# Holding a DMA queue for four loads, and moving two small loads behind the matmuls, in a long-convolution and MLP kernel

## The chip, the cores and the metric

The program runs on one core of one Trainium2 chip. A core has a matrix engine (TensorE, PE in the profile, with its weight loads as PEld), three engines for elementwise work (VectorE or DVE, ScalarE or ACT, GpSimd or POOL) and a queue engine (SyncE or SP). All of them run their own list of instructions in order and wait for each other through semaphores. SP, ACT and POOL can start DMAs; a DMA is issued by an instruction in the engine's own list, and whatever stands behind that instruction waits until it has been accepted. The metric is the time of one execution on the device in microseconds (us), lower is better.

## The reference

The inputs are a sequence of 2048 positions with 640 channels, all in float32. What is computed:

```python
mod = (silu(c) @ w_mod).reshape(1, 6, 1, 640)
sa, ca, ga, sb, cb, gb = (mod[:, i] for i in range(6))
h = layernorm(x) * (1 + ca) + sa                 # x is A_q
# A: short causal convolution of k (4 taps), times v, then a causal
#    convolution over all 2048 positions with ssm_k (by FFT of length 4096)
kv = shift_conv(k, shift_k) * v
y  = irfft(rfft(kv, 4096) * rfft(ssm_k, 4096))[:2048] + kv * ssm_D
x  = x + ga * (h * y)
h  = layernorm(x) * (1 + cb) + sb
# B: dense layer, squared relu, dense layer (640 -> 1728 -> 640)
x  = x + gb * (relu(h @ w1 + b1) ** 2 @ w2 + b2)
```

## The kernel before, in words

The 640 channels are worked on in five blocks of 128 (the loop `for b in range(NB)`). In each block the long convolution is done as a transform in two steps on TensorE. `unit_a(b, i, g)` (matmuls at L354) is the first step, on a quarter g of the block, for the filter (i = 1, tile half `pt[b][:, 1]`) or for the product kv (i = 0, `pt[b][:, 0]`). `early_h` and `front` (matmuls at L369) are the second step; `front` also multiplies the two spectra (DVE L140, POOL L143 and L146). `back` (L435), `unit_t` (L499) and `unit_y` (L510) go back to positions. While one block goes through the second step and back, the first step of the next block, the short convolution of the block after it (`kv_k`, `kv_s`, `kv_v`, `kv_m`) and the layernorm statistics (`stats1`) are placed between its matmuls. After the five blocks comes the MLP, with PE nearly filled.

The kv of a block is computed with channels on partitions and written to a DRAM tile `kv_d` (L257), and read back by `load_x(b, n)` (L204) in another layout, in n pieces; one piece has as many rows as one call of `unit_a(b, 0, g)` needs. So in block 0, with four pieces, the four calls `unit_a(0, 0, g)` can begin one after the other as the pieces land. The same holds for block 1; blocks 2 to 4 load theirs in one piece. `load_h` (L196) brings the filter, `load_gb` and `load_gi` (L798, L330) the tables of the two steps, `kv_load` (L216) the rows of k and v, `part_load` (L308) rows of `w_mod` and `q_load` (L915) rows of q.

Nearly all DMAs are issued by SP, in the order of the program text; this order, like that of every engine, is fixed by `keep_order` at the end. An entry of a table (`at(FS(b, j), ...)`, `at(GS(b, s), ...)`) says at which of the 28 places of a block a piece of work is put; equal places keep the order in which they were entered. ACT issues a few small ones itself: taps, one table and parts of `ssm_D` at the start, then `c` (tile `ct`, L849) and the table `ca` of the last step (`ca_d`, L850). In the program text these two stand between the last `early_h` of the prologue and the four calls `unit_a(0, 0, g)`, whose results ACT copies out of PSUM (L135). `c` is first read by `mod_start` at place GS(0, 0), the table by `unit_y` at GS(0, 3).

The text of the prologue around the change, in order: `load_x(0, 4)`, `unit_a(0, 1, 3)`, `load_gb(3)`, two pairs of `kv_load` with `load_gi`, `load_h(1)`, two more `load_gi`, six `early_h`, the two DMAs on ACT, four `unit_a(0, 0, g)`. In block 1 `load_x(1, 4)` stands at GS(0, 6), and the next DMA of SP behind it is `part_load(2, 1)` at the same place.

## Time and profile before

| | us |
|---|---|
| median of three runs | 711.5 |
| lowest and highest of them | 709.77, 716.64 |
| the profiled execution | 714.4 |
| its span, first to last instruction | 712.6 |
| PE busy in the span | 669.5 (94%) |
| PE weight loads busy | 639.2 (90%) |
| DVE, ACT, POOL busy | 335.7, 330.7, 295.5 |

The mean clock granted to TensorE in that execution is 0.983 of full speed. In the profile's second part the span is cut into 40 slices of some 17.8 us; a digit is a busy share in tenths. PE stands at 9 in nearly all slices from the sixth on, and is lower in the first five (6, 5, 9, 8, 9); the DMA engines stand at 9, 8, 7, 7, 7 there, and are nearly idle in the last third. The three runs lie 1% apart. The first 100 us are the part in which the change lies; all times of events below are counted from the start of the span.

### The profile page before, as it was taken

To read this page: it belongs to the slowest core of one execution; us is meant where nothing else is said; L and a number is where in the kernel's file an instruction comes from. 1 tells how busy PE (TensorE), PEld (TensorE's weight loads), DVE (VectorE), ACT (ScalarE), POOL (GpSimd) and SP (SyncE) were. 2 spreads that over 40 slices of the span, in tenths; PEclk is the share of its full clock that TensorE was granted. 3 is DMA by queue.
4 is the path that set the end of the run, shared out by engine and by line. 5 is a ranking of instruction groups with operands and counts; after the bars stand their busy time and mean duration, and the time that the engine had idled before them with its cause. 6 is when DMAs were issued, how large, how long until landed. Compare 5 with 4: busy or idle time off the path is not lost.

```text
span 712.6 us, 21026 instructions
## 1 busy us (share of the span) xinstructions
PE 669.5 (94%) x9164; PEld 639.2 (90%) x9164; DVE 335.7 (47%) x661; ACT 330.7 (46%) x685; POOL 295.5 (41%) x338
## 2 busy tenths in 40 slices
PE   6598989979899989999999999999999999999997
PEld 5587878769789879789999999999999999999996
DVE  5255755746887588769831232222312313312313
ACT  4426545766883896557533323323333333233221
POOL 1042026147944977933542522422514415325213
PEclk9989989999999999999999999999999999999999
DMA  9877795969475275238320020020020110200101
GB/s 250 239 209 236 210 271 165 257 184 247 101 194 150 69 207 153 78 89 243 106 73 3 1 75 1 1 75 1 3 75 1 38 38 1 75 1 1 39 1 38
DMA packets 88721, 74.76 MB, mean 105 GB/s; under 512 B 19250, under 2 KB 73906, under 8 KB 88628
## 3 DMA queue, kind: packets, MB, share of 16 engines
q1 hardware_dynamic: 86672, 72.86, 36.1%
q8 instruction: 72, 1.18, 0.7%
q10 hardware_dynamic: 1892, 0.54, 0.3%
q14 instruction: 21, 0.17, 0.1%
q0 software_dynamic: 64, 0.01, 0.0%
HBM read 58.98 MB, written 14.42 MB: 103 GB/s over the span
## 4 chain that ended last, share of the span: by engine, by line
PE 79%; DVE 9%; ACT 4%; DMA 3%; issue 2%; POOL 2%; SPq 0%; DVEq 0%; POOLq 0%; ACTq 0%
PE acc L763 26%; PE h L693 25%; PE x L369 5%; PE qp L435 4%; PE h L369 4%; DVE KV L239 3%; PE y L510 3%; PE pa L354 3%; PE t L499 1%; PE h L684 1%; PE xtp L658 1%; PE kt L227 1%; ACT KV L468 1%; ACT q L135 1%; DVE s L270 1%
## 5 line engine op out<-in xcount | busy, mean ns | idle before, releaser
L140 POOL TENSOR_TENSOR mtmp<-mtmp 128x256 f32<-128x256 f32 x112 | 72.1, 643 | 242.3 <-ACT mtmp L725 234.5
L693 PE MATMUL h<-xt,w_S 128*128 128x256 f32 x1290 | 166.9, 281 | 0.2 <-DVE w_S L146 0.2
L693 PEld LDWEIGHTS h<-xt,w_S 128*128 128x128 f32 x1290 | 161.2, 190 | 0.4 <-DVE w_S L146 0.4
L763 PE MATMUL acc<-w_S,hring 128*128 128x320 f32 x960 | 156.8, 311 | 0.2 <-DVE hring L146 0.2
L146 DVE TENSOR_TENSOR hring<-mtmp,hring 128x256 fp32r<-128x256 f32 x112 | 64.9, 579 | 189.9 <-ACT hring L135 189.8
L763 PEld LDWEIGHTS acc<-w_S,hring 128*128 128x128 f32 x960 | 141.8, 188 | 0.7 <-DVE hring L146 0.7
L725 ACT ACTIVATE mtmp<-h,b1t 128x256 f32<-128x256 f32 x104 | 49.4, 475 | 177.8 <-PE h L693 172.3
L135 ACT ACTIVATE hring<-mtmp 128x256 fp32r<-128x256 f32 x112 | 46.7, 417 | 46.1 <-POOL mtmp L140 44.6
L354 PE MATMUL pa<-wx,p 64*64 64x64 f32 x2560 | 52.3, 232 | 13.9 <-DMA p<-kv_d 3.8
L354 PEld LDWEIGHTS pa<-wx,p 64*64 64x64 f32 x2560 | 45.9, 145 | 21.6 <-issue 11.6
L135 ACT ACTIVATE a<-pa 128x512 f32<-128x512 f32 x80 | 43.7, 604 | 28.9 <-PE pa L354 28.9
L510 PE MATMUL y<-wx,wx 128*64 128x64 f32 x1280 | 47.1, 227 | 6.5 <-ACT wx L135 4.9
L140 DVE TENSOR_TENSOR wx<-x,wx 128x512 f32<-128x512 f32 x64 | 40.8, 681 | 25.3 <-PE x L369 14.6
L510 PEld LDWEIGHTS y<-wx,wx 128*64 128x64 f32 x1280 | 41.7, 140 | 11.4 <-ACT wx L135 5.7
L146 POOL TENSOR_TENSOR we<-wx 128x256 f32<-128x256 f32 x20 | 15.9, 793 | 79.9 <-DVE wx L140 77.9
L369 PE MATMUL x<-a,gb 128*64 128x128 f32 x640 | 44.1, 283 | 1.2 <-ACT a L135 1.1
L143 POOL TENSOR_TENSOR wm<-wm,wm 128x640 f32<-128x640 f32 x20 | 31.8, 1590 | 28.5 <-ACT wm L312 28.3
L660 DVE TENSOR_SCALAR we<-xtp,cbs 128x256 f32<-128x256 f32 x35 | 19.0, 543 | 51.8 <-PE xtp L658 51.8
L239 DVE SCALAR_TENSOR_TENSOR KV<-kt,tap,KV 128x511 f32<-128x511 f32 (+2 forms) x48 | 35.4, 738 | 15.1 <-ACT ktail L135 13.1
L369 PEld LDWEIGHTS x<-a,gb 128*64 128x64 f32 x640 | 38.5, 143 | 2.1 <-ACT a L135 1.3
L135 ACT ACTIVATE q<-qp 128x512 f32<-128x512 f32 (+1 forms) x40 | 21.3, 584 | 35.2 <-PE qp L435 35.2
L369 PE MATMUL h<-a,gb 128*64 128x128 f32 x512 | 36.2, 285 | 0.0
(140 smaller groups left out, 1029.6 us busy)
## 6 DMA issues: line engine op xcount, KB each, us to landing
wm<-in_w_mod_dram SPq DMA_DIRECT2D x25, 320.0 KB, 5.1
KV<-in_A_k_dram SPq DMA_DIRECT2D x20, 256.0 KB, 5.3
KV<-in_A_v_dram SPq DMA_DIRECT2D x20, 256.0 KB, 4.2
xp<-in_A_q_dram SPq DMA_DIRECT2D x5, 1024.0 KB, 9.5
out_dram<-x SPq DMA_DIRECT2D x14, 320.0 KB, 2.9
w1s<-in_B_w_dram SPq DMA_DIRECT2D x13, 320.0 KB, 3.7
w2s<-in_B_w_dram SPq DMA_DIRECT2D x13, 320.0 KB, 3.6
kv_d<-KV SPq DMA_DIRECT2D x16, 256.0 KB, 4.0
```

The source lines that it names most:

```text
L135: act.activation(o, i, AF.Copy)
L140: eng.tensor_mul(o, a, b)
L143: eng.tensor_add(o, a, b)
L146: eng.tensor_sub(o, a, b)
L239: dve.scalar_tensor_tensor(o, x, tap[:, b, t : t + 1], o, op0=ALU.mult, op1=ALU.add)
L354: pe.matmul(t[e][64 * r : 64 * r + 64, g].rearrange("p m d -> p (m d)"), pt[b][l, i, 8 * q + g, :], cw[l, r], start=True, stop=True,)
L369: pe.matmul(t[64 * a : 64 * a + 64, s + r], gb[:, g, r, a], AX[b][i][:, 2 * g + a], start=True, stop=True,)
L435: pe.matmul(t[a][:, u], gi[l, 4 * j + u, r], w[r][l, u % 2], start=(r == 0), stop=(r == 1),)
L510: pe.matmul(y[64 * h : 64 * h + 64, 4 * (g % 2) + i].rearrange("p c l d -> p (c l d)"), tss[g][:, i, 64 * r : 64 * r + 64], ca[:, r, h], s ...
L693: pe.matmul(hps[n, f][:m], WI[1, f][:, a, b], XT[n][:, x, b], start=(b == 0 and i == 0), stop=(b == NB - 1 and i == 2),)
L725: act.activation(r[:m], h[:m], AF.Relu, bias=b1t[:m, f : f + 1])
L763: pe.matmul(acc[2 * s + i], h[:, a, s * P : (s + 1) * P], w[:, y, i * 320 : (i + 1) * 320], start=(f == 0 and ti == 0), stop=(f == NF - 1 ...
```

## The change

Three things change.

1. All DMAs of SP go through a new function `sp_dma`. It issues the DMA, and when the list `behind` holds a name, the DMA just issued gets a dependence on that earlier instruction, with a semaphore: it is not issued before the named DMA has landed.
2. `load_x` puts the name of its third piece (index 2 of four) in that list for blocks 0 and 1. So the next DMA of SP after each of these two loads waits until three quarters of x have landed, and everything behind it in SP's order waits too. In block 0 that DMA is `load_gb(3)`, in block 1 it is `part_load(2, 1)`. The fourth piece is issued ahead of the wait.
3. The DMAs of `c` and of the last table stand behind the four `unit_a(0, 0, g)` in ACT's order, not ahead of them.

```diff
+HOLD = {0: 2, 1: 2}
...
+    behind = []
+
+    def sp_dma(o, i):
+        sp.dma_start(o, i)
+        if behind:
+            info = mybir.DependencyInfo(mybir.DependencyClass.Sync, mybir.DependencyReason.DATA)
+            tc.add_manual_dep(nc.cur_bb.bb.instructions[-1], behind.pop(), info, reason="place in time")
...
     def load_x(b, n=1):
         w = DG // n
         for i in range(n):
-            sp.dma_start(
+            sp_dma(
                 pt[b][:, 0, i * w : (i + 1) * w],
                 xsrc[:, b * DG + i * w : b * DG + (i + 1) * w, :],
             )
+            if i == HOLD.get(b):
+                held = nc.cur_bb.bb.instructions[-1].name
+        if b in HOLD:
+            behind.append(held)
...
     for j in range(6):
         early_h(0, j)
+    for g in range(4):
+        unit_a(0, 0, g)
     act.dma_start(ct, c.rearrange("o (b p) -> p (o b)", p=P))
     act.dma_start(ca, ca_d.rearrange("p (r h n) -> p r h n", r=2, h=2))
-    for g in range(4):
-        unit_a(0, 0, g)
```

All other `sp.dma_start` of the kernel become `sp_dma` with the same arguments.

More of the change, by code (lines that the diff above doesn't have):

```diff
@@ L203, in load_x @@
         for i in range(n):
-            sp.dma_start(
+            sp_dma(
                 pt[b][:, 0, i * w : (i + 1) * w],
@@ L215, in kv_load @@
         for w, src in ((0, k), (1, v)):
-            sp.dma_start(t[:, w], src[rows, cols].rearrange("(t p) d -> p t d", p=P))
+            sp_dma(t[:, w], src[rows, cols].rearrange("(t p) d -> p t d", p=P))
     kt = {}
@@ L256, in kv_m @@
         dve.tensor_mul(acc, kt[1], acc)
-        sp.dma_start(kv_d[b * P : (b + 1) * P, h * 512 : (h + 1) * 512], acc)
+        sp_dma(kv_d[b * P : (b + 1) * P, h * 512 : (h + 1) * 512], acc)
     st1 = sb.tile([P, NL, 2], F32, tag="st1", name="st1")
@@ L307, in part_load @@
         t = parts[j, b] = sb.tile([P, D], F32, tag="STG", name=f"wm_{j}_{b}", bufs=4)
-        sp.dma_start(t, w_mod[b * P : (b + 1) * P, j * D : (j + 1) * D])
+        sp_dma(t, w_mod[b * P : (b + 1) * P, j * D : (j + 1) * D])
     def part_scale(j, b):
@@ L329, in load_gi @@
         src = gi_d.rearrange("p (g r n) -> p g r n", g=16, r=2)
-        sp.dma_start(gi[:, 4 * i : 4 * i + 4], src[:, 4 * i : 4 * i + 4])
+        sp_dma(gi[:, 4 * i : 4 * i + 4], src[:, 4 * i : 4 * i + 4])
     AX, QT = {}, {}
@@ L457, in load_xp @@
         t = sb.tile([P, NL, P], F32, tag=f"XP{b % 2}", name=f"xp_{b}")
-        sp.dma_start(t, q[:, b * P : (b + 1) * P].rearrange("(l p) d -> p l d", p=P))
+        sp_dma(t, q[:, b * P : (b + 1) * P].rearrange("(l p) d -> p l d", p=P))
         XPt[b] = t
@@ L546, in finish_add @@
         add(pool, x[:, js], x[:, js], u[:, js])
-        sp.dma_start(
+        sp_dma(
             x1_d[4 * j * P : (4 * j + 4) * P, b * P : (b + 1) * P].rearrange("(l p) d -> p l d", p=P),
@@ L572, in w_load @@
         if kind == 1:
-            sp.dma_start(
+            sp_dma(
                 s[:, 0 : 5 * m].rearrange("p (k f) -> p k f", k=NB),
@@ L585, in w_load @@
             for j in range(P // m):
-                sp.dma_start(s[j * m : (j + 1) * m], w2[f * P : f * P + m, :])
+                sp_dma(s[j * m : (j + 1) * m], w2[f * P : f * P + m, :])
             d = WI[2, f] = dst.rearrange("p (h x) -> p h x", h=2)
@@ L636, in load_x1 @@
             X1t[n] = x1_tile(n)
-            sp.dma_start(
+            sp_dma(
                 X1t[n], x1_d[n * CH : (n + 1) * CH, :].rearrange("(l p) d -> p l d", p=P)
@@ L785, in mlp_out @@
                 add(dve if s else pool, X1t[n][:, s], t, X1t[n][:, s])
-                sp.dma_start(out[l * P : (l + 1) * P, :], X1t[n][:, s])
+                sp_dma(out[l * P : (l + 1) * P, :], X1t[n][:, s])
                 continue
@@ L792, in mlp_out @@
                 add(dve if s else pool, X1t[n][:, s, o], t[:, o], X1t[n][:, s, o])
-                (act if i else sp).dma_start(out[l * P : (l + 1) * P, o], X1t[n][:, s, o])
+                (act.dma_start if i else sp_dma)(out[l * P : (l + 1) * P, o], X1t[n][:, s, o])
     def load_gb(i):
         src = gb_d.rearrange("p (g r a f) -> p g r a f", g=16, r=2, a=2)
-        sp.dma_start(gb[:, 4 * i : 4 * i + 4], src[:, 4 * i : 4 * i + 4])
+        sp_dma(gb[:, 4 * i : 4 * i + 4], src[:, 4 * i : 4 * i + 4])
     act.dma_start(tap, shift_k.rearrange("(b p) t -> p b t", p=P))
@@ L814, in load_h0 @@
     def load_h0(i):
-        sp.dma_start(pt[0][:, 1, 8 * i : 8 * i + 8], hsrc[:, 8 * i : 8 * i + 8, :])
+        sp_dma(pt[0][:, 1, 8 * i : 8 * i + 8], hsrc[:, 8 * i : 8 * i + 8, :])
         skip(0, 8 * i, 8 * i + 8)
@@ L914, in q_load @@
     def q_load(t, l0, n):
-        sp.dma_start(t, q[l0 * P : (l0 + n) * P, :].rearrange("(l p) d -> p l d", p=P))
+        sp_dma(t, q[l0 * P : (l0 + n) * P, :].rearrange("(l p) d -> p l d", p=P))
         for i in range(n):
@@ L1005, in b1_load @@
     def b1_load():
-        sp.dma_start(b1t[:, : NF - 1], b1[: (NF - 1) * P].rearrange("(f p) -> p f", p=P))
-        sp.dma_start(b1t[:64, NF - 1 : NF], b1[(NF - 1) * P :].rearrange("(f p) -> p f", f=1))
+        sp_dma(b1t[:, : NF - 1], b1[: (NF - 1) * P].rearrange("(f p) -> p f", p=P))
+        sp_dma(b1t[:64, NF - 1 : NF], b1[(NF - 1) * P :].rearrange("(f p) -> p f", f=1))
     at(GS(3, 13), b1_load)
@@ L1016, in gate_load @@
         for b in range(NB):
-            sp.dma_start(g5[0][:, b], w_mod[b * P : (b + 1) * P, 5 * D : 6 * D])
+            sp_dma(g5[0][:, b], w_mod[b * P : (b + 1) * P, 5 * D : 6 * D])
     def gate_vector():
@@ L1041, in b2_load @@
         row1b[0] = sb.tile([P, D], F32, tag="row1", name="gb2row")
-        sp.dma_start(row1b[0], b2.rearrange("(o d) -> o d", o=1).to_broadcast([P, D]))
+        sp_dma(row1b[0], b2.rearrange("(o d) -> o d", o=1).to_broadcast([P, D]))
     at(FS(4, 4), gate_load)
```

## The prediction

> **What bounds the kernel now.** I read the page first, then the waits of PE, then SP's and PE's instructions between 20 and 110 us in order of time, and last the clock by stretches.

> ```profile
> span 712.6 us, 21026 instructions
> PE 669.5 (94%) x9164; PEld 639.2 (90%) x9164; DVE 335.7 (47%) x661; ACT 330.7 (46%) x685; POOL 295.5 (41%) x338
> q8 instruction: 72, 1.18, 0.7%
> ```

> PE is the bound as a whole, with 43 us of the span in which it is idle. So a change of DMAs can pay only where PE stands still or runs at a lower clock. The chain of work around the first load of x shows such a place (start, length, what it was):

> ```profile
> 24.81 4.83 DMA p<-kv_d
> 29.77 3.70 PE pa L354 x148
> 33.47 2.32 issue
> 35.80 1.33 PE pa L354 x37
> 37.15 1.09 ACT a L135 x2
> 38.28 1.97 PE x L369 x16
> 40.26 1.71 PE eh L369 x16
> 41.96 1.30 PE x L369 x16
> ...
> 98.90 0.87 PE x L369 x16
> ```

> The second piece of x lands at 29.64 and ends a wait; then comes a stop of 2.32 us that no semaphore explains; then a copy of ACT; and then 16 matmuls take 1.97, 1.71 and 1.30 us that take 0.87 at 98.90. In order of time for PE, ACT and SP:

> ```profile
> 24.39 3.35 SPq L204 DMA_DIRECT2D p<-kv_d  x4
> 24.81 0.46 ACTq L849 DMA_DIRECT2D ct<-in_c_dram  x1
> 25.31 0.54 ACTq L850 DMA_DIRECT2D wx<-in_ca_dram  x1
> 27.70 1.16 PE L354 MATMUL pa<-wx,p 64*64 64x64 f32 x64 [2.94 <-DMA p<-kv_d]
> 27.78 1.42 SPq L798 DMA_DIRECT2D gb<-in_gb_dram  x1
> 29.77 3.70 PE L354 MATMUL pa<-wx,p 64*64 64x64 f32 x150 [0.91 <-DMA p<-kv_d]
> 34.81 8.16 SPq L330 DMA_DIRECT2D gi<-in_gi_dram  x2
> 35.80 1.40 PE L354 MATMUL pa<-wx,p 64*64 64x64 f32 x42 [2.32 <-issue]
> 42.01 0.60 ACT L135 ACTIVATE hs<-eh 128x512 f32<-128x512 f32 x1 [3.78 <-PE eh L369]
> ```

> The clock by stretches (length, busy time of PE, PEld, DVE, ACT, POOL, granted clock, DMA share, GB/s):

> ```profile
> 32.47:35.88 3.41, 1.09 (x66) 0.95 (x63) 0.00 (x0) 1.48 (x3) 0.00 (x0) 1.00 1.10 343
> 35.88:42.70 6.82, 5.73 (x84) 5.54 (x85) 1.29 (x2) 1.68 (x3) 0.96 (x2) 0.50 1.13 278
> ```

> A stretch of 3.41 us with PE busy for 1.09 was followed by 6.82 us at half the clock. The second piece's wait (0.91), the stop (2.32) and the half clock are what this change can take away.

> **Block 0, c and the table moved.** The DMA view of 26 to 29 us, of the third piece alone, of 33.0 to 34.5, of `gb(3)` and of the first `gi` (us to landing at the end):

> ```profile
> q10 hardware_dynamic: 800, 0.13, 28.4%
> ...
> p<-kv_d SPq DMA_DIRECT2D x1, 256.0 KB, 5.3
> ...
> q8 instruction: 1, 0.02, 4.9%
> ...
> gb<-in_gb_dram SPq DMA_DIRECT2D x1, 512.0 KB, 5.5
> ...
> gi<-in_gi_dram SPq DMA_DIRECT2D x1, 512.0 KB, 7.2
> ```

> Queue 10 is ACT's: its 800 packets took 28.4% of 16 engines for 3 us, or 0.85 us of all engines, in the middle of x. Without them the second piece lands at 29.64 - 0.85 = 28.8, the third, issued near 25.4 (the second of the four began at 24.81, the last ended at 27.74) and landed 5.3 later at 30.7, at 29.9; with the same 1.1 between pieces the fourth moves from some 31.8 to 31.0. So the second call of `unit_a` starts at 28.9, not 29.77.

> **Block 0, the held queue.** The loads held are issued from 27.78 on, behind all of x in the same queue. The third piece landed 1.1 us after the second with 0.5 MB of table already issued behind it, so I cost the hold at nothing for x itself. [...]

> The stop is such a fetch, as I read it: 72 packets of 1.18 MB in all are 16 KB each, and 18328 matmuls and weight loads by 72 are 255, so a packet holds some 127 pairs. PE stopped 64 + 150 = 214 pairs after 27.70; if a block is asked for when the one before it is begun, it was asked for 87 pairs after 27.70, 23 pairs into the second call, at 30.3, and came 5.5 us later. [...] The packet itself took 4.9% of 16 engines for 1.5 us, 1.18 us, and is over by 34.5, so at least 1.3 us pass from its end to PE's start. In the changed kernel it is asked for at 28.9 + 0.6 = 29.5, when only the rest of x is under way, and the queue behind x is empty. Bounds: at best it needs its own 1.2 us and there is no stop; at worst it needs 5.5 us again and PE resumes at 35.0. I take it that it starts when x is through, at 31.0, and PE resumes 1.2 + 1.3 later at 33.5. Nothing else is late there: the second to fourth calls take 3.70 us from 28.9 to 32.6 for the first 150 pairs. Then 42 pairs at full clock take 42 x 1.16/64 = 0.8, ACT's copy and gaps 1.15: the first spectrum starts at 35.45 where it was 38.28, or **2.8 us sooner**.

> **Block 0, the clock.** From 38.28 to the end of the second `eh` near 44.1 four groups (the fourth at full clock again) took 5.8 us; at full clock they take 3.65 (a first one of 1.02, three of 0.87). With PE stopped until 33.5, the stretch from 32.47 holds some 1.3 us of PE work, still too little, so I let one stretch of 3.41 be halved and not two: 0.43 us at full clock, 3.41 at some 1/1.6, and 1.1 left, so the end is at 40.4. That is 3.7 us sooner instead of 2.8. If the clock stays up it is 5.0; if it is halved throughout, 2.8.

> **Block 0, what is late next.** The wait delays SP's next issue from 27.78 to 30.0. `load_gb(3)` needs 5.5 us before, so lands by 35.5 and is read by the `eh` that starts at about 36.4. The tables and k, v behind it were landing at a rate set by the DMA engines (share 1.13), not by the issue: the two last `gi` needed 8.16 us to be accepted. The DMA engines can lose the 2.2 us of the wait at most; I take 1, as the fourth piece is under way for half of it. The first `gi`, issued after 29.2 (the end of the `gb` issue), landed 7.2 us later, by 38; with 2.2 more it is there by 40.2, and its first use, `qp`, comes behind the four groups above, past 40.4. c and the table cost ACT 0.46 + 0.54 us after its last copy, in the 3.78 us in which it waited before 42.01. That is cover, if they are accepted at once.

> **Block 1.**

> ```profile
> 79.32 2.94 SPq L204 DMA_DIRECT2D p<-kv_d  x4
> 82.72 1.96 SPq L308 DMA_DIRECT2D wm<-in_w_mod_dram  x2
> 85.45 0.47 SPq L216 DMA_DIRECT2D KV<-in_A_k_dram  x1
> 86.56 0.63 SPq L257 DMA_DIRECT2D kv_d<-KV  x1
> 90.53 0.92 PE L354 MATMUL pa<-wx,p 64*64 64x64 f32 x24 [2.02 <-DVE KV L256]
> 92.29 1.33 PE L354 MATMUL pa<-wx,p 64*64 64x64 f32 x36 [0.84 <-issue]
> 97.17 0.71 PE L227 MATMUL kt<-ident,KV 128*128 128x128 f32 x4
> 97.91 0.69 ACT L228 ACTIVATE KV<-kt,tap 128x512 f32<-128x512 f32 x1 [1.74 <-PE kt L227]
> ...
> p<-kv_d SPq DMA_DIRECT2D x1, 256.0 KB, 5.7
> KV<-in_A_k_dram SPq DMA_DIRECT2D x1, 256.0 KB, 8.2
> kv_d<-KV SPq DMA_DIRECT2D x1, 256.0 KB, 8.6
> ```

> The four units here wait for DVE, not for x, so the hold wins nothing by x. It can end the stop of 0.84, again a fetch in a loaded queue. It costs 3.4 us of SP: the third piece, issued near 80.4 (four issues in 2.94 us from 79.32) and 5.7 under way, lands at 86.1, and the loads of `w_mod` issued at 82.72 go out then; behind them stand q, k and v of the next part, a write of kv, and the filter of block 2. The k issued at 85.45 lands at 93.7 and is used at 97.17, the write issued at 86.56 lands at 95.1 and must have landed before ACT writes its buffer at 97.91. Margins of 3.5 and 2.8 against at most 3.4: between 0.84 won and 0.6 lost. I take 0.

> **The sum.** 714.4 for the profiled execution, 712.6 of it span and 1.8 around it, less 3.7 is 710.7. The median of the runs shown is 2.9 below that execution; some of this may be a shorter stop in the same place, so off the median I take 3.5: 711.5 - 3.5 = **708.0**. The unknowns at their best ends (fetch in time, 33.5 to 32.6; clock up throughout, 3.7 to 5.0; 0.84 in block 1) add 3.0 and give 704.8; nothing but the 0.85 gives 710.7.

> **Rivals.** First, *the fetch stays late*: it waits for something other than SP's backlog and needs 5.5 us as before. Then PE resumes at 35.0, all that follows is 0.8 to 1.0 sooner and the clock is halved as before: 710.6. For it: the stop of 0.84 came with as much behind it; against it: both stops lie where the DMA engines were full (share 1.10 in 32.47 to 35.88). [...]

> Second, *slower: ACT is stuck*. c and the table are now issued at about 34.6, when SP's queue is full; SP itself then needed 8.16 us for two DMAs, until 43.0. No row has ACT issuing into such a stretch: bounds 1.0 us (0.46 + 0.54 at 24.81) and that until 43.0 and beyond. I take 1.0, the row of the same DMAs. If ACT waits for the same space as SP, it is free at some 43.5, and the first `eh` is copied 1.5 us later than at 42.01; PE runs on for the buffers it has and stands from some 39 on. Half a clock after that costs two stretches, 1.5 to 3 us. That is 713.0, with nothing of the gain left. It decides from the point where ACT is free later than 42.

> Third, *the hold of block 1 bites*: data land 3.4 later while PE comes there earlier than before because a fetch or the clock was better. Then PE waits for k and gets a halved stretch; 1.7 us (half of 3.41) go, 709.7.

> **How the numbers follow.** Forecast 0.52, fetch late 0.2, ACT stuck 0.18, block 1 0.1. The forecast's own range is 704.8 to 710.7. To hold 8 in 10 it must reach up to the stuck ACT, with its cost open by 1, and a little below the best ends, since the halved stretches can fall otherwise: 704.0 to 714.0. One per cent is 7 us, about what three runs that lie 1% apart can tell from no change. Faster by more needs the best ends of all terms: 0.13. Slower by more needs ACT stuck and a longer stop after it: 0.10. The rest, 0.77, is within 1%.

> **What would show it.** In the changed profile: the second `unit_a` of x starting about 0.9 us after 27.7 plus its own 1.16 instead of 2.07 us; SP's next issue at about 30; a stop of some 1 us for `pa` instead of 2.32; `x` at L369 near 35.5; one halved stretch or none before 43; ACT's two DMAs of half a microsecond each. I am wrong if ACT's DMAs take several us, if the stop stays above 2 us, or if PE waits for `KV` from DRAM near 92.

## The result and the profile after

The changed kernel takes 705.43 us in the median of 22 executions (700.07 to 712.27); the kernel before, run beside it, 710.83 us (707.8 to 719.08, 22 executions). The ratio is 0.992, with a 95% interval from 0.9895 to 0.9944: faster by 0.6 to 1.1%. A second comparison of the same program later (e9 below) gave 0.9975 (0.9944 to 1.0007).

The execution that was profiled (712.27) is one of the few executions that lie more than 1.5% above the fastest of their program and that ratios and means leave out, so another profile of the same program, of an execution of 711.05 us, stands beside it further down. Page of the profile after, first line:

```profile
span 710.5 us, 21027 instructions
```

The chain of work after, around x (start, length, what it was; L368 and L383 are L354 and L369 of before):

```profile
27.51 1.16 PE pa L368 x64
28.71 1.16 PE pa L368 x64
29.91 1.68 PE pa L368 x84
31.59 0.84 issue
32.43 0.83 PE pa L368 x39
...
34.42 1.09 PE x L383 x16
35.52 0.87 PE eh L383 x16
36.39 0.87 PE x L383 x16
37.27 0.87 PE eh L383 x16
```

The second unit starts at 28.71 instead of 29.77; the stop without a semaphore is 0.84 instead of 2.32; the first spectrum starts at 34.42 instead of 38.28; and its four groups, 16 matmuls each, run at full speed. The second `eh` ends at 38.14, 6.0 us before the 44.1 of the kernel before. In order of time for SP, ACT and PE, the lines that answer the prediction's questions on the two queues and on block 1:

```profile
29.80 0.35 SPq L138 DMA_DIRECT2D gb<-in_gb_dram  x1
33.35 0.40 ACTq L865 DMA_DIRECT2D ct<-in_c_dram  x1
33.90 0.59 ACTq L866 DMA_DIRECT2D wx<-in_ca_dram  x1
35.97 10.78 SPq L138 DMA_DIRECT2D gi<-in_gi_dram  x2
...
87.70 0.57 PE L368 MATMUL pa<-wx,p 64*64 64x64 f32 x23 [1.70 <-DVE KV L270]
88.65 9.70 SPq L138 DMA_DIRECT2D KV<-in_A_k_dram  x1
91.16 1.33 PE L368 MATMUL pa<-wx,p 64*64 64x64 f32 x37 [2.89 <-issue]
```

SP's next issue is at 29.80, as the hold has it. ACT's two DMAs take 0.40 and 0.59 us and are accepted by 34.5, before SP begins the two that take it 10.78; whether ACT would be stuck beside them, e1 shows (under the rivals below). In block 1 PE stops for 2.89 us where it stopped for 0.84 before. The clock by stretches (length, busy PE, PEld, DVE, ACT, POOL, granted clock, DMA share, GB/s):

```profile
25.84:29.25 3.41, 1.70 (x100) 1.62 (x104) 0.00 (x0) 0.56 (x2) 0.00 (x0) 1.00 1.27 240
29.25:32.66 3.41, 2.52 (x142) 2.27 (x138) 0.00 (x0) 2.70 (x6) 0.00 (x0) 1.00 0.80 188
32.66:36.07 3.41, 2.28 (x71) 2.14 (x65) 0.44 (x1) 1.08 (x2) 0.00 (x0) 1.00 0.87 276
...
87.27:90.69 3.42, 0.57 (x23) 0.44 (x24) 1.38 (x4) 0.00 (x0) 0.00 (x0) 1.00 1.00 317
90.69:94.10 3.41, 2.94 (x53) 2.82 (x54) 0.00 (x0) 1.08 (x2) 0.00 (x0) 0.50 1.08 331
```

None of the stretches shown around x is followed by one at half clock; the one around the stop in block 1 is (0.57 busy, then 0.50). So of the 6.0 us won by 38 this execution keeps 2.1 in its span, 712.6 to 710.5. What of that is the change and what is the single execution is a question for the experiments.

### The profile page after: what moved, and what is told of

Its sections match the earlier page's. It is cut to its first block, busy times and chain, and to the rows that moved or that the text cites. A ratio compares the mean times of both kernels' runs of the same rounds, so it can differ in the third digit from the quotient of the medians.

```text
span 710.5 us, 21027 instructions
## 1 busy us (share of the span) xinstructions
PE 666.4 (94%) x9164; PEld 636.5 (90%) x9164; DVE 336.3 (47%) x661; ACT 330.6 (47%) x685; POOL 295.1 (42%) x338
## 3 DMA queue, kind: packets, MB, share of 16 engines
q8 instruction: 72, 1.18, 0.7%
## 4 chain that ended last, share of the span: by engine, by line
PE 81%; DVE 8%; ACT 5%; issue 3%; DMA 2%; POOL 1%; DVEq 0%; POOLq 0%; SPq 0%; ACTq 0%
PE acc L777 26%; PE h L707 25%; PE qp L449 5%; PE x L383 4%; PE h L383 4%; PE y L524 4%; PE pa L368 4%; DVE KV L253 2%; PE t L513 2%; PE h L698 1%; PE xtp L672 1%; ACT a L145 1%; DVE kacc L253 1%; ACT q L145 1%; ACT KV L482 1%
## 5 line engine op out<-in xcount | busy, mean ns | idle before, releaser
L368 PEld LDWEIGHTS pa<-wx,p 64*64 64x64 f32 x2560 | 44.7, 140 | 20.7 <-issue 12.1
L368 PE MATMUL pa<-wx,p 64*64 64x64 f32 x2560 | 51.1, 228 | 12.6 <-issue 3.9
L145 ACT ACTIVATE a<-pa 128x512 f32<-128x512 f32 x80 | 43.5, 599 | 26.7 <-PE pa L368 26.3
L153 POOL TENSOR_TENSOR wm<-wm,wm 128x640 f32<-128x640 f32 x20 | 31.8, 1589 | 28.3 <-ACT wm L326 28.1
L383 PE MATMUL x<-a,gb 128*64 128x128 f32 x640 | 41.9, 274 | 1.2 <-ACT a L145 1.1
L253 DVE SCALAR_TENSOR_TENSOR KV<-kt,tap,KV 128x511 f32<-128x511 f32 (+2 forms) x48 | 35.5, 739 | 15.3 <-ACT ktail L145 13.3
L383 PEld LDWEIGHTS x<-a,gb 128*64 128x64 f32 x640 | 36.2, 137 | 2.3 <-ACT a L145 1.3
L383 PE MATMUL h<-a,gb 128*64 128x128 f32 x512 | 35.0, 280 | 0.0
## 6 DMA issues: line engine op xcount, KB each, us to landing
KV<-in_A_k_dram SPq DMA_DIRECT2D x20, 256.0 KB, 5.8
KV<-in_A_v_dram SPq DMA_DIRECT2D x20, 256.0 KB, 4.6
kv_d<-KV SPq DMA_DIRECT2D x16, 256.0 KB, 4.2
```

Of the source, the lines that this page charges most:

```text
L145: act.activation(o, i, AF.Copy)
L153: eng.tensor_add(o, a, b)
L253: dve.scalar_tensor_tensor(o, x, tap[:, b, t : t + 1], o, op0=ALU.mult, op1=ALU.add)
L368: pe.matmul(t[e][64 * r : 64 * r + 64, g].rearrange("p m d -> p (m d)"), pt[b][l, i, 8 * q + g, :], cw[l, r], start=True, stop=True,)
L383: pe.matmul(t[64 * a : 64 * a + 64, s + r], gb[:, g, r, a], AX[b][i][:, 2 * g + a], start=True, stop=True,)
```

## The experiments

All of them compute the whole reference; only e5 adds work, which nothing reads. L138 in their rows is `sp_dma`.

### The change in its parts: e1 to e4

e1, from the kernel before: c and the table moved, nothing held.

```diff
-    act.dma_start(ct, c.rearrange("o (b p) -> p (o b)", p=P))
-    act.dma_start(ca, ca_d.rearrange("p (r h n) -> p r h n", r=2, h=2))
     for g in range(4):
         unit_a(0, 0, g)
+    act.dma_start(ct, c.rearrange("o (b p) -> p (o b)", p=P))
+    act.dma_start(ca, ca_d.rearrange("p (r h n) -> p r h n", r=2, h=2))
```

> Only the two DMAs of ACT are moved; nothing is held. Theory (fetch and backlog): x lands sooner by the 0.85 us that c and the table took, so the second unit_a of x starts near 28.9 and not 29.8, but the stop of PE after 214 pairs stays at 2 us or more, because SP's backlog is what delays the fetch; the first spectrum of x (L369 in the kernel before) starts near 37.3, some 1 us sooner than 38.28, and the clock is halved as before; time 709 to 710.5 beside 710.8. [...]

e2, from the changed kernel: only block 0 held, the two DMAs back in their old place.

```diff
-HOLD = {0: 2, 1: 2}
+HOLD = {0: 2}
...
+    act.dma_start(ct, c.rearrange("o (b p) -> p (o b)", p=P))
+    act.dma_start(ca, ca_d.rearrange("p (r h n) -> p r h n", r=2, h=2))
     for g in range(4):
         unit_a(0, 0, g)
-    act.dma_start(ct, c.rearrange("o (b p) -> p (o b)", p=P))
-    act.dma_start(ca, ca_d.rearrange("p (r h n) -> p r h n", r=2, h=2))
```

> Only block 0 is held; c and the table stay where they were. Theory: the pieces of x land as before (second unit_a of x near 29.8), but the fetch is served while the queue is empty, so the stop falls from 2.3 to under 1 us and the spectrum of x starts near 36.5; the halved stretch after it shrinks or goes; time 707 to 709. [...]

e3, from the changed kernel with the two DMAs back in their old place, as in e2, but with block 1 held in place of block 0:

```diff
-HOLD = {0: 2, 1: 2}
+HOLD = {1: 2}
```

> Only block 1 is held. Theory: x is not what PE waits for there, so nothing is won; the loads let go at once come when the next fetch is asked for, so the stop of 0.84 us near 92 grows to 2 to 3 us; time 711 to 713 beside 710.8. Rival (the hold serves block 1 as it serves block 0): the stop near 92 goes, time 709.5 to 710.

e4, the changed kernel without the hold of block 1:

```diff
-HOLD = {0: 2, 1: 2}
+HOLD = {0: 2}
```

> The change without its hold in block 1. Theory: all of block 0's gain (spectrum of x near 34.4), and the stop near 91 is about 1 us and not 2.9, so it is 1 to 2 us faster than the whole change: 703.5 to 704.5 where the change has 705.4. Rival: the hold in block 1 carries part of the gain, and this is slower than the whole change by 1 to 2: 706.5 to 707.5.

Measured, beside 35 executions of the kernel before (711.48):

| | median us | ratio (95%) |
|---|---|---|
| e1, move alone | 711.53 | 1.0011 (0.9978 to 1.0043) |
| e2, hold of block 0 alone | 708.84 | 0.9973 (0.9942 to 1.0004) |
| e3, hold of block 1 alone | 711.86 | 1.0001 (0.9967 to 1.0034) |
| e4, move and hold of block 0 | 706.02 | 0.9936 (0.9906 to 0.9966) |

PE's instructions in order of time, in e1:

```profile
29.27 3.70 PE L354 MATMUL pa<-wx,p 64*64 64x64 f32 x150 [0.21 <-DMA p<-kv_d]
35.42 1.44 PE L354 MATMUL pa<-wx,p 64*64 64x64 f32 x42 [2.45 <-issue]
37.94 1.33 PE L369 MATMUL x<-a,gb 128*64 128x128 f32 x10 [1.08 <-ACT a L135]
```

and in e2, e3 and e4, one fence each:

```profile
32.94 0.85 PE L368 MATMUL pa<-wx,p 64*64 64x64 f32 x42 [0.90 <-issue]
34.93 1.09 PE L383 MATMUL x<-a,gb 128*64 128x128 f32 x16 [1.14 <-ACT a L145]
```

```profile
34.78 0.85 PE L368 MATMUL pa<-wx,p 64*64 64x64 f32 x42 [2.29 <-issue]
36.77 1.98 PE L383 MATMUL x<-a,gb 128*64 128x128 f32 x16 [1.14 <-ACT a L145]
```

```profile
33.05 0.85 PE L368 MATMUL pa<-wx,p 64*64 64x64 f32 x42 [1.29 <-issue]
35.04 1.09 PE L383 MATMUL x<-a,gb 128*64 128x128 f32 x16 [1.14 <-ACT a L145]
```

What decides is when PE resumes after the stop. Without the hold of block 0 that is at 35.80 (before), 35.42 and 34.78; with it, at 32.94 and 33.05. In e1 the second unit does start 0.5 us sooner, at 29.27, but the stop grows to 2.45 and the spectrum is only 0.34 us sooner: a unit that starts sooner waits longer for the same late thing. That fits a move that alone is worth nothing that can be measured, against the expected 0.85 and more.

Between e2 and e4, which ran on the same chip, the means differ by 2.4 us (0.6 to 4.3 at 95%), so moving the two DMAs seems to pay once the queue is held. A second such pair, e9 and e10 below, gave 0.6 (-1.3 to 2.6). The sign is likely, the size open.

The hold of block 1 does nothing that can be measured, alone (1.0001) or on top of the rest (e4 0.9936, the whole change 0.992 and 0.9975): neither the 1 to 2 us that I had expected from leaving it out nor the gain that the rival gave it is seen. PE's waits between 75 and 100 us, in e3, show a trace of the price that the third rival named:

```profile
...
PE kt L241 <- DMA KV<-in_A_k_dram: 0.5, 1, 0.5
```

0.5 us of waiting for k from DRAM, and no stop of `pa` without a semaphore, where 2 to 3 us were expected. Of the three profiles with block 1 held, two (e3, e9) have no such stop and one has 2.89. Without that hold it is 0.84 in before, none in e1 and e6, 0.5 in e2, 1.4 in e4, 0.6 in e7, 1.3 in e10 and 0.7 in e11 (e5 and e8 have another order of work). That is no basis for a verdict.

### Is the stop an instruction fetch? e5

If PE stops because the next block of its instructions has not come, the stop is tied to the count of instructions and moves when some are put ahead. From the kernel before:

```diff
+    tpad = ps.tile([P, 8, 32, 2], F32, tag="T", name="pad", bufs=2)
+    for i in range(40):
+        pe.matmul(
+            tpad[0:64, i % 8].rearrange("p m d -> p (m d)"), pt[0][0:64, 1, i % 8, :], cw[0:64, 0], start=True, stop=True
+        )
     for g in range(4):
         unit_a(0, 0, g)
```

> The kernel before with 40 more pairs of weight load and 64x64 matmul on PE, into a tile that nothing reads, in the idle time before the first unit_a of x. Theory (the stop is the fetch of the next 256 instructions): it comes 40 pairs sooner in the text, after 174 and not 214 pairs of the four unit_a of x, 22 before the end of the third call. Rival (the stop waits for data of the last piece, or for something else at the fourth call): it stays after 214 pairs, in the fourth call.

One execution, 717.81 us. PE in order of time:

```profile
25.28 4.82 PE L853 MATMUL pad<-wx,p 64*64 64x64 f32 x79
...
30.00 2.61 PE L354 MATMUL pa<-wx,p 64*64 64x64 f32 x132
34.23 2.02 PE L354 MATMUL pa<-wx,p 64*64 64x64 f32 x121 [1.62 <-issue]
37.43 0.65 PE L369 MATMUL x<-a,gb 128*64 128x128 f32 x6 [1.18 <-ACT a L135]
40.03 0.71 PE L369 MATMUL x<-a,gb 128*64 128x128 f32 x9 [1.95 <-issue]
```

I had counted 40 added pairs; the trace shows 80 matmuls (79 in the row above, one among the first of `pa`), two for each of these float32 calls, and the page of before has as many weight loads as matmuls (9164 of both). The stop then has to come 214 - 80 = 134 pairs into `pa` instead of 214. It comes after 3 (in a group of their own) + 132 = 135. The next one comes 121 + 6 = 127 pairs after that, in the middle of a group of `x` whose data are there, where before has none. So the stop belongs to a place in the list of instructions, here 127 pairs after the one before it, and not to a tile.

The DMA traces say the same in another way. The 16 KB packets of queue 8, of the kind `instruction` in the DMA view, come once per such block: in before, from the packet that begins at 314.30 to the one that begins at 699.83, there are 23 of them to 2947 matmuls and 2946 weight loads, 256 instructions or 128 pairs to a packet. And in the thirteen profiles PE has 64 stops of over 0.2 us without a semaphore after the first 25 us. Every one of them ends 1.2 to 1.7 us after a packet of queue 8 has ended. In the kernel before that packet lasts from 33.17 to 34.35 and PE resumes at 35.80; in the profile after it lasts from 29.64 to 30.92 and PE resumes at 32.43.

### How long must the queue be held? e6, e7, e11

Both from e4: the hold ends with the first piece of x (e6, the first diff), or with all four (e7, the second).

```diff
-HOLD = {0: 2}
+HOLD = {0: 0}
```

```diff
-HOLD = {0: 2}
+HOLD = {0: 3}
```

> As the change in block 0 (c and the table moved), but the queue is held for the first piece alone, so the other loads go out near 27.5 and not 29.8, ahead of the time near 29 at which the fetch is asked for. Theory: the stop of PE in the fourth unit_a is back at 2 us or more. Rival (any pause of the queue, or the moved DMAs, carry it): the stop stays near 1 us.

> As the change in block 0, but the queue is held for all four pieces, so the other loads go out near 31. Theory: the fetch is served as with three quarters, the stop is 0.8 to 1.3 us, and the tables come 1 us later without a wait of PE before 50. Rival (the fetch comes with the first free moment after the hold ends): the stop grows by the 1 us of the longer hold.

e6, one execution, 711.53 us (SP, then PE, in order of time):

```profile
27.36 1.03 SPq L138 DMA_DIRECT2D gb<-in_gb_dram  x1
34.93 1.10 PE L368 MATMUL pa<-wx,p 64*64 64x64 f32 x42 [2.22 <-issue]
37.12 1.97 PE L383 MATMUL x<-a,gb 128*64 128x128 f32 x16 [1.09 <-ACT a L145]
```

e7, one execution, 703.51 us:

```profile
30.93 0.34 SPq L138 DMA_DIRECT2D gb<-in_gb_dram  x1
32.52 0.85 PE L368 MATMUL pa<-wx,p 64*64 64x64 f32 x42 [0.82 <-issue]
34.51 1.09 PE L383 MATMUL x<-a,gb 128*64 128x128 f32 x16 [1.13 <-ACT a L145]
```

With SP let go at 27.36, before the block is asked for by the prediction's way of counting (near 29), the old stop is back, 2.22. With SP held until 30.93 it is 0.82, about what it is in the changed kernel. The clearest evidence is this pair: same program, same order, only the moment of release differs, and the fetch follows it. The packets of queue 8 for this block agree in all the profiles with this order of work: they begin at 33.17, 32.90, 32.19 and 32.48 in before, e1, e3 and e6, and between 29.64 and 30.98 in after, e2, e4, e7, e9, e10 and e11, where three or four pieces are held for. The packet lasts 1.0 to 1.3 us in all of them, so the delay lies ahead of it. What the runs don't separate is SP's backlog from the load on the DMA engines: the hold takes away both.

Part of the stop stays. 128 pairs of `pa` take 128 x 1.16/64 = 2.3 us at full clock; in the changed kernel PE went on at 32.43, 3.3 us after the place 86 pairs into `pa` (29.1) at which the block was asked for, if it was asked for when the one before it was begun; that is an assumption, and no run shows the moment. Of these 3.3 us 0.5 lie ahead of the packet, 1.3 in it and 1.5 behind it. So at full clock 0.8 to 1.3 us of stop are left in the profiles with the hold.

e7's single time calls for more executions:

> c and the table moved, the queue held in block 0 until all four pieces have landed, nothing held in block 1. Theory: the stop in the fourth unit_a is 0.8 as in its first look, the floor of a fetch behind 128 pairs; as fast as the change or up to 1.5 us faster: 704 to 706. Rival (1 us more of hold makes the tables late and PE waits for them before 60): 707 to 709.

708.88 us; ratio to the kernel before, run beside it, 0.9977 (0.9943 to 1.0011). Holding for all four pieces isn't seen to be better than for three, and e7's 703.5 was one lucky execution. The time is the rival's, but not its cause: in the profile PE waits for no table before 60. Nor does PE stop there within the 256 pairs of `pa`; the units ran at half clock from 28.70 to 32.11, as in e9 below.

### A short queue throughout: e8

If a backlog on SP's queue is what delays the fetch, a queue that never holds more than three DMAs should end the other stops too. From e4:

```diff
+    issued = []
+
     def sp_dma(o, i):
         sp.dma_start(o, i)
+        issued.append(nc.cur_bb.bb.instructions[-1].name)
+        if 3 < len(issued) < 120:
+            info = mybir.DependencyInfo(mybir.DependencyClass.Sync, mybir.DependencyReason.DATA)
+            tc.add_manual_dep(nc.cur_bb.bb.instructions[-1], issued[-1 - 3], info, reason="place in time")
```

> As the change in block 0, and each of the first 120 DMAs of SP waits until the third one before it has landed, so that never more than three are under way. Theory (SP's backlog delays fetches): the stops of 0.3 to 2.9 us that no semaphore explains between 30 and 215 us mostly go (some 6 us in the profile before), PE waits somewhat longer for data instead, and the time is 702 to 705 beside 710.8. Rival (fetches are late by chance or by the engine load, not by the length of the queue): the stops stay, and the waits come on top: 707 to 712.

721.95 us, ratio 1.0151 (1.0113 to 1.0189): 1.5% slower than before. PE's waits between 25 and 330 us (L374 is `unit_a`, L530 `unit_y`, L455 `back`, L247 the short convolution of k):

```profile
PE y L530 <- issue: 4.5, 3, 1.7
PE pa L374 <- issue: 3.8, 4, 2.1
...
PE qp L455 <- DMA gi<-in_gi_dram: 2.0, 1, 2.0
...
PE kt L247 <- DMA KV<-in_A_k_dram: 1.2, 1, 1.2
```

The stops without a semaphore are still there (`pa` 3.8 us in the same view of before, too; `y` 0.8 there and 4.5 here), and waits for tables and for k have come on top. So my theory holds at the place that was changed and not as a rule for the kernel. Three DMAs of 256 to 512 KB may still be a backlog, where the hold of block 0 leaves nothing but the rest of x in flight; or the load on the engines counts and not the length of the queue, as the rival says. That wasn't tried further.

### The whole and the hold alone once more: e9, e10

> The whole change once more, beside the next two on the same chip, for a comparison of the three. Theory (block 0 carries the gain, block 1's hold adds nothing and may cost 1): a spectrum of x near 34.5, the stop in the fourth unit_a near 0.9, and 705 to 706.5 beside 711 for the kernel before. Rival (the gain was a matter of that day's executions): 709 or more.

> The hold of block 0 alone, c and the table left in the middle of x. Theory (c and the table are worth the time that they take among x, and no more than the clock that hangs on it): slower than the hold with the moved DMAs by 0.5 to 2, so 706 to 708.5. Rival (the two halves only work together): 709.5 to 711, near the kernel before.

e9, the changed kernel again: 706.94, ratio 0.9975 (0.9944 to 1.0007). e10, the same as e2: 708.97, ratio 0.9967 (0.9934 to 0.9999). Both times lie between the ranges of theory and rival. SP's and PE's rows of e9, and its clock by stretches:

```profile
28.22 6.05 PE L368 MATMUL pa<-wx,p 64*64 64x64 f32 x256 [2.84 <-DMA p<-kv_d]
30.50 0.34 SPq L138 DMA_DIRECT2D gb<-in_gb_dram  x1
35.41 1.09 PE L383 MATMUL x<-a,gb 128*64 128x128 f32 x16 [1.14 <-ACT a L145]
```

```profile
24.82:28.23 3.41, 0.57 (x13) 0.36 (x8) 0.00 (x0) 0.93 (x2) 0.00 (x0) 1.00 0.77 160
28.23:31.64 3.41, 3.41 (x128) 3.41 (x132) 0.00 (x0) 1.08 (x2) 0.00 (x0) 0.50 1.04 168
31.64:35.06 3.42, 2.51 (x140) 2.23 (x132) 0.00 (x0) 2.85 (x6) 0.00 (x0) 1.00 0.67 209
```

Here PE runs through all 256 pairs without a listed stop: it was at half clock while the block was fetched, and came to the end of its instructions later. The first spectrum starts at 35.41, 1 us later than in the profile after: the first piece came 0.7 us later (28.22 in place of 27.51), and the units ran partly at half clock.

### What part is clock, what part is stops

Every execution has a time and a mean granted clock. Over those of e1 to e4 and e8 to e11, with the first comparison of the changed kernel and the executions of before that were run beside e1 to e4 and e8 to e11 (those of the first comparison have no clock on record), one hundredth more of mean clock goes with 4.4 us less, within each kernel. The program with the move and the hold of block 0 (the changed kernel, e4 and e9: 44 executions, mean 706.25, clock 0.9892) is 3.9 us (2.9 to 4.9) below that of before (63, 710.19, clock 0.9857). 0.0035 of clock is worth 1.5 of that; 2.4 (1.7 to 3.1) remain at equal clock. I read the 2.4 us as time in which PE no longer stands; that is an inference from the sum and not a measurement of stops. This is worked out from executions of several comparisons and assumes that these agree, so it is rougher than the ratios.

## Why the prediction was right

**The number.** 708.0 was forecast for 711.5; measured were 705.43 against 710.83 and 706.94 against 710.53. In place of 3.5 us the two comparisons give 5.4 and 3.6, and all executions together 3.9. The direction and the place hold; that the size comes so close is in part luck, since two errors of opposite sign lie in it (the clock, and what becomes of the gain behind block 0, both below).

**c and the table moved: the term was mis-sized.** The second unit was to start at 28.9; it started at 28.71. But "2.8 us sooner" counted 0.85 of it as a gain of the move. e1 shows that alone it gives nothing that can be measured (1.0011, 0.9978 to 1.0043); its stop of 2.45 takes the gain back, since the fetch sets the end. The prediction knew that the fetch would decide, and yet gave, with "nothing but the 0.85", 710.7 as the upper end of its own range, where nothing at all was the right end.

**The held queue costs x nothing: right.** The units of x start 1.2 us apart (27.51, 28.71, 29.91), where the prediction had 1.1 between pieces. What the hold gives is not x but the fetch: with SP let go at 27.36 its packet begins at 32.48 and PE stops for 2.22 us (e6), with SP held until 30.93 the stop is 0.82 (e7). How the DMA engines divide their time between SP's loads and the fetch was not shown.

**The stop is a fetch, and it follows what SP has let go: right, shown by e5, e6, e7 and the packets of queue 8.** The size of the stop was given as about 1 us and is 0.84, 0.90, 1.29 and 0.82 with the hold (after, e2, e4, e7; none where the units ran at half clock, in e9, e10 and e11), 2.32, 2.45, 2.29 and 2.22 without (before, e1, e3, e6). The 5.5 us in before from the request (30.3 by the prediction's count) to resuming are about 2.9 ahead of the packet, 1.2 in it and 1.45 behind it; 30.3 rests on the assumption that a block is asked for when the one before it is begun, which no run shows. The assumption that the fetch starts only "when x is through, at 31.0" was 1 us too late: in the profile after, PE resumes at 32.43 where 33.5 was forecast, and the packet of the block began at 29.64, 1.2 us before the last piece landed. DMA view of 29.6 to 31.1 after, and the same kind of row as in the prediction:

```profile
q8 instruction: 1, 0.02, 5.3%
```

**The first spectrum 2.8 us sooner: too little by 0.5 on average.** 35.45 was forecast; the three profiles of the program (after, e4, e9) have 34.42, 35.04 and 35.41. The 3.70 us that the sum gives the second to fourth calls were read from a row that ran mostly at half clock: in before the stretch from 29.05 to 32.47 is halved (0.50, last section). At full clock the 150 pairs take 2.9 us (28.71 to 31.59 after). The forecast isn't hurt by it, since PE then waits for the fetch.

**The clock: the wrong one of three cases.** One halved stretch was expected over the spectra after the stop, for 3.7 us in all. In the profiles with the hold of block 0 none lies there, so the case "the clock stays up" (5.0) was the right one: 6.0 and 5.0 us were won by the end of the second `eh` (38.14 after, 39.1 in e9). One profile of before is a thin base for that; over all profiles this end lies at 38.1 to 40.1 with the hold (after, e2, e4, e7, e9, e10, e11) and at 42.1 to 44.1 without (before, e1, e3, e6). The step that failed is "still too little": with PE going on 1.1 us sooner than assumed and the stop at 0.84, the two stretches around it hold 2.52 and 2.28 us of PE work, not 1.3, and neither was followed by half a clock. What the sum has no term for is a halved stretch earlier, over the units themselves, behind the wait for the first piece: before has one, the profile after doesn't, and e9, e10 and e11 have it again.

**The gain of block 0 was forecast as the gain of the kernel.** It isn't: 5 to 6 us at 39, some 3.9 at the end. In the profile after, the 2.89 us of stop in block 1 with its half clock take back part of it. Whether later stops come because data were moved, or fall as they do from one execution to the next, isn't settled. They do differ much between two profiles of the same program: between 25 and 330 us PE's waits without a semaphore are 9.3 us in after and 1.9 in e9, and 5.9 in before.

**What is late next.** The first table `gi` was to be there 0.2 us ahead of its use; in the profile after `qp` waits 0.2 us for it, which changes nothing in the sum.

**Rivals.** The fetch stays late: fell (e6 shows what that would look like). ACT is stuck behind SP: fell. In the profile after, ACT's DMAs are through before SP gets stuck; in e1 they come 1.2 us into a pair of DMAs that takes SP 6.84 us, and are accepted in 0.40 and 0.54:

```profile
35.70 6.84 SPq L330 DMA_DIRECT2D gi<-in_gi_dram  x2
36.90 0.40 ACTq L851 DMA_DIRECT2D ct<-in_c_dram  x1
37.34 0.54 ACTq L852 DMA_DIRECT2D wx<-in_ca_dram  x1
```

The hold of block 1 bites: its mechanism is seen once, 0.5 us in e3, its price isn't.

## What to carry to other kernels

Where PE stops with no semaphore to explain it, count matmuls, and look when the packets of the instruction queue end: if stops come a fixed number of instructions apart (127 pairs in e5) and each ends shortly after such a packet (1.2 to 1.7 us in these profiles), read them as instruction fetches, and ask what other DMAs are in flight before the packet begins; that can be changed. Here a queue held until three pieces of x have landed, not one, takes most of the stop away (0.84 in the profile after, 2.22 in e6), while a queue kept short throughout cost more than it won (1.5% slower). And move transfers out of a load's way only after asking what is late next: here that was the fetch, and the move by itself won nothing that could be measured (1.0011).

## What the runs showed of the hardware that was not expected

```profile
25.64:29.05 3.41, 1.16 (x64) 1.05 (x64) 0.00 (x0) 0.17 (x1) 0.00 (x0) 1.00 1.07 223
29.05:32.47 3.42, 2.70 (x101) 2.73 (x105) 0.00 (x0) 1.61 (x4) 0.00 (x0) 0.50 1.19 277
```

The spread of the times (702.25 to 716.21 for the kernel before in one comparison) goes along with the mean clock (0.999 and 0.978 in these two executions). By these rows I estimate that a wait of about 2 us is worth 2 us in some executions and 1.1 to 1.7 more in others (the 128 pairs that e9 does in a halved 3.41 us take 2.3 at full clock; 1.7 is half of 3.41), and a single profile can't price it.
